# A gated recurrence with a routed expert block on Trainium2: the second expert's rows gathered in quarters and turned by VectorE instead of TensorE

## Chip, cores and metric

The kernel runs on one core of a Trainium2 chip, in one launch, in float32 throughout. The metric is device time in microseconds (us). A run's time is that of the whole execution; beside it stands the span of one profiled execution, from its first to its last instruction.

## What is computed

```python
# q, k, v, a_re, a_im: (4, 8, 768, 48); w_gate (384, 8); w1 (8, 384, 1024); w2 (8, 1024, 384)
for t in range(S):                       # recurrence per batch and head, complex decay
    S = a_n[t] * S + outer(k[t], v[t])   # a_n: a with its magnitude limited to 0.999
    y[t] = q[t] @ S.real
x = y.transpose(0, 2, 1, 3).reshape(3072, 384)
logits = x @ w_gate
e = argmax(logits, axis=1)               # one of 8 experts for each row
gate = softmax(logits)[row, e]
out = gate * (relu(x @ w1[e]) @ w2[e])   # each row through its own expert only
```

## The kernel before, in words

**First part, attention.** The recurrence is computed in six chunks of 128 time steps for each of the four batches, 24 steps in all, on TensorE (PE), with decays and rotations prepared by ScalarE (ACT) and VectorE (DVE). Each step writes 128 finished rows of 384 numbers to a scratch tensor `xd` in device memory and adds to the routing: which expert a row goes to, and its rank there. An explicit table of due times (`WHEN`) gives the order in which a list scheduler places this part.

**Second part, experts.** The eight experts are taken in order of their number of rows, and the order's positions are called places (0 to 7). Place i has room for `CAPS[i]` rows: 448, 416, 416, 408, 400, 384, 376, 360. For each place, in the loop at lines 949 to 961:

- `load_w(i)` (line 588) loads w1 of that expert into `wa` and w2 into `wb`, 1.5 MB each, from SyncE's queue (SP).
- `gather(i, ...)` (line 604) fetches the rows from `xd` into `xg` by indirect DMAs, which GpSimd (POOL) issues one by one.
- `turn(i, ...)` (line 625) puts the rows' 384 features on the partitions, in `xt`.
- `expert(i, ...)` (line 673) computes, per place, `hps` = w1 part times `xt` (8 groups of three products), relu into `ht` (odd groups by ACT, line 686, even ones by DVE, line 688), `yps` = `ht` times w2 for each tile of up to 128 rows, the gate (line 708), and `scatter` (line 654), an indirect DMA of POOL that writes the rows to the output.

In the program a float32 product is two matmul instructions: place 0's last two tiles show 48 of them for 8 groups of three products. A transpose on TensorE is one.

Places come in two kinds, separated by the constant `SQ`. A place below `SQ` is gathered in tiles of 128 whole rows and turned by TensorE: for each of the three blocks of 128 features, one transpose per tile into PSUM (line 643) and one copy to SBUF (line 650, ACT or DVE). A place from `SQ` on is gathered in quarters: four partitions hold a row, 96 numbers in each, so that one indirect DMA brings 32 rows, and one VectorE instruction (line 633) turns the whole place in squares of 32 by 32. Its w1 is loaded in four DMAs of 32 partitions each, since the features then lie in another order over the partitions. The indices of the quarters (`tok4`) come from `squares()` (line 569), which runs for all places whatever `SQ` is.

```python
if i < SQ:                                              # gather, lines 609 to 614
    view, w = xd[0:rows, :], DM
    parts = [(min(P, c1 - t * P), t, tok[:, i, t : t + 1]) for t in range(t0, t1)]
else:
    view, w = xd.rearrange("n (a c) -> (n a) c", a=4), DM // 4
    parts = [(P, j, tok4[:, i, j // 4, j % 4 : j % 4 + 1]) for j in range(4 * t0, -(-c1 // Q4))]
...
if i >= SQ:                                             # load_w, lines 593 to 595
    w = w1[ds(ev, 1)].rearrange("o (a k j) f -> a j (o k) f", a=4, k=KD)
    parts = [(slice(a * Q4, (a + 1) * Q4), w[a]) for a in range(4)]
```

**Order and buffers around the change.** Place 0's first two tiles are worked in the attention part (`early`, line 725), its last two at the start of the loop. The buffers of even and of odd places are two sets of one each (`EP[0]`, `EP[1]`), so place 2's rows can be gathered only when place 0's have been turned. `load_w(1)` waits for place 0's turn (line 948). `turn(i + 1)` is called in the middle of `expert(i)`, behind its relus; the VectorE form is bound to come after the last relu of that place on DVE (`T["held"]`, line 637). VectorE also runs a check of the inputs' range in six pieces (`in_range`, line 916), two passes of 1536 columns each (`junk`, line 923), whose data SP loads into `rc` (line 920). POOL takes its DMAs strictly in the order of the program: place 0's last tiles, place 1's rows, the first scatter, place 2's rows with the second scatter among them, place 3's rows.

Of the kernel before, what the change touches and what calls it, by code (L numbers as in the profile page):

```python
# [22 lines left out]
LN_CAP = math.log(0.999)  # L23
A_MIN = 0.61
T_MAX = 1.5
SQ = 2
Q4 = 32
CAPS = (448, 416, 416, 408, 400, 384, 376, 360)

# [9 lines left out]
def kernel(  # L39
# [40 lines left out]
    def const(shape, name, dt=FP):  # L80
        return cp.tile(shape, dt, name=name)
# [381 lines left out]
    own0 = const([P, 1], "own0", I32)  # L463
    tok = const([P, SQ, CT], "tok", I32)
    tok4 = const([P, E, CT, 4], "tok4", I32)
# [46 lines left out]
    def to_read(f, o):  # L512

        ts(out=o, in0=f, scalar1=-1.0, scalar2=0.0, op0=OP.add, op1=OP.max)
# [37 lines left out]
    def gates_of_places():  # L552
        f = small([P, E, CT], "fi")
        by_place(f, 2)
        to_read(f, f)
        nc.vector.tensor_copy(out=tok, in_=f[:, 0:SQ])
        T["fi"] = f
# [30 lines left out]
    def load_w(i, after=None):  # L588
# [3 lines left out]
        parts = [(slice(0, P), w1[ds(ev, 1)].rearrange("o (k p) f -> p (o k) f", p=P))]  # L592
        if i >= SQ:
            w = w1[ds(ev, 1)].rearrange("o (a k j) f -> a j (o k) f", a=4, k=KD)
# [9 lines left out]
    def gather(i, t0, t1, rows=N):  # L604
# [3 lines left out]
        c1 = min(CAPS[i], t1 * P)  # L608
        if i < SQ:
            view, w = xd[0:rows, :], DM  # L610
# [14 lines left out]
    def turn(i, t0, t1, ps, end=None):  # L625
# [4 lines left out]
        c0, c1 = t0 * P, min(CAPS[i], t1 * P)  # L630
        if i >= SQ:
            j1 = -(-c1 // Q4)
# [615 lines left out]
```

## Time and profile before

| What | us |
|---|---|
| time, median of 3 runs | 550.28 |
| lowest and highest of the 3 | 550.03, 550.4 |
| the profiled execution's own time | 549.1 |
| its span | 547.4 |
| PE busy with matmuls, in the span | 521.0 |
| DVE busy | 288.6 |
| ACT busy | 215.0 |
| POOL busy | 124.0 |

The span begins at 0; times below are microseconds from there. Attention ends at about 270, and the expert part fills the rest. A line of the timeline gives the start, the length, the engine, the line of the kernel, the operation, what it writes and reads, how many instructions were merged, and in brackets how long the engine sat idle before and what released it. A line of the chain of waits gives the start, the length and the work: it follows what ended last back to what released it. "DMA to landing" is the time from the start of an issuing instruction to the moment its data is in place.

### The profile page before, as it was taken

To read this page: it belongs to the slowest core of one execution; us is meant where nothing else is said; L and a number is where in the kernel's file an instruction comes from. 1 tells how busy PE (TensorE), PEld (TensorE's weight loads), DVE (VectorE), ACT (ScalarE), POOL (GpSimd) and SP (SyncE) were. 2 spreads that over 40 slices of the span, in tenths; PEclk is the share of its full clock that TensorE was granted. 3 is DMA by queue.
4 is the path that set the end of the run, shared out by engine and by line. 5 is a ranking of instruction groups with operands and counts; after the bars stand their busy time and mean duration, and the time that the engine had idled before them with its cause. 6 is when DMAs were issued, how large, how long until landed. Compare 5 with 4: busy or idle time off the path is not lost.

```text
span 547.4 us, 8302 instructions
## 1 busy us (share of the span) xinstructions
PE 521.0 (95%) x3166; PEld 372.0 (68%) x3166; DVE 288.6 (53%) x586; ACT 215.0 (39%) x324; POOL 124.0 (23%) x152
## 2 busy tenths in 40 slices
PE   3979979999999999999999999999999999999995
PEld 2756858877888889898885755555555555565663
DVE  5388688678788888697375211271452113111210
ACT  6787888977668974564310110110201111000000
POOL 3000000000000000000034774743716416322101
PEclk9999989999999999999999999999999999999998
DMA  9987692859555935701829976485964334641001
GB/s 164 187 112 109 111 127 33 167 83 175 98 95 99 150 75 110 126 25 29 297 89 308 313 208 152 144 314 108 323 160 145 105 74 140 158 145 42 27 2 42
DMA packets 167495, 73.49 MB, mean 134 GB/s; under 512 B 148861, under 2 KB 160151, under 8 KB 167448
## 3 DMA queue, kind: packets, MB, share of 16 engines
q1 hardware_dynamic: 162744, 63.12, 52.9%
q0 software_dynamic: 4704, 9.76, 6.1%
q8 instruction: 27, 0.44, 0.4%
q14 instruction: 20, 0.16, 0.1%
HBM read 63.34 MB, written 9.73 MB: 134 GB/s over the span
## 4 chain that ended last, share of the span: by engine, by line
PE 84%; issue 6%; DVE 4%; DMA 2%; ACT 2%; POOLq 0%; POOL 0%; ACTq 0%
PE yps L69 22%; PE hps L69 22%; PE tp L332 8%; PE yt L69 7%; PE at L69 7%; PE dk L69 4%; PE cst L69 3%; PE csl L69 3%; PE xb L69 3%; PE warm L69 2%; DMA xg<-xd,tok 1%; PE sp L69 1%; DMA ar<-in_a_re_dram 1%; PE tp L643 1%; DVE fg L283 1%
## 5 line engine op out<-in xcount | busy, mean ns | idle before, releaser
L69 PE MATMUL yps<-wb,ht 128*128 128x384 f32 (+6 forms) x464 | 134.2, 487 | 0.0
L69 PE MATMUL hps<-xt,wa 128*128 128x416 f32 (+7 forms) x432 | 132.7, 465 | 0.0
L69 PEld LDWEIGHTS hps<-xt,wa 128*128 128x128 f32 x432 | 79.8, 190 | 49.8 <-issue 24.8
L69 PEld LDWEIGHTS yps<-wb,ht 128*128 128x128 f32 (+6 forms) x464 | 75.1, 175 | 55.9 <-issue 8.6
L616 POOL DMA_INDIRECT xg<-xd,tok x83 | 85.9, 1035 | 99.3 <-PE tp L332 40.3
L686 ACT ACTIVATE ht<-hps 128x416 f32<-128x416 f32 (+7 forms) x36 | 16.8, 468 | 149.9 <-PE hps L69 138.8
L708 DVE TENSOR_SCALAR y<-yps,gate 128x384 f32<-128x384 f32 (+1 forms) x23 | 14.2, 617 | 101.7 <-PE yps L69 101.7
L69 PE MATMUL at<-qt,kt 96*128 96x128 f32 x384 | 54.0, 280 | 0.3 <-DVE am L340 0.3
L655 POOL DMA_INDIRECT out_dram<-y,row x28 | 29.2, 1044 | 105.4 <-DVE y L708 44.9
L688 DVE TENSOR_SCALAR ht<-hps 128x416 f32<-128x416 f32 (+7 forms) x36 | 18.9, 525 | 63.9 <-PE hps L69 63.7
L261 POOL DMA_DIRECT2D ai<-cd x4 | 3.4, 841 | 210.2 <-ACT R L175 99.5
L69 PEld LDWEIGHTS at<-qt,kt 96*128 96x128 f32 x384 | 47.6, 191 | 4.1 <-issue 1.6
L69 PE MATMUL yt<-am,v 128*48 128x128 f32 x384 | 42.7, 281 | 0.6 <-DVE am L340 0.6
L340 DVE TENSOR_TENSOR am<-at,tri 128x512 f32<-128x512 f32 x48 | 33.0, 688 | 18.6 <-PE at L69 18.5
L69 PE MATMUL yt<-qt,G 96*48 96x128 f32 x320 | 35.7, 274 | 0.0
L718 ACT COPY z<-yps 32x384 f32<-32x384 f32 (+3 forms) x13 | 6.1, 471 | 74.2 <-PE yps L69 74.1
L332 PE MATMUL tp<-ident,K 128*96 128x128 f32 x192 | 33.4, 284 | 1.2 <-DVE K L323 0.8
L69 PEld LDWEIGHTS dk<-v,K 128*96 128x96 f32 x320 | 32.6, 166 | 2.1 <-issue 1.0
L332 PE MATMUL tp<-ident,Q 128*96 128x128 f32 x192 | 33.4, 277 | 0.0
L69 PE MATMUL dk<-v,K 128*96 128x48 f32 x320 | 33.2, 242 | 0.2 <-DVE G L371 0.2
L334 ACT COPY kt<-tp 96x512 f32<-96x512 f32 x48 | 27.9, 582 | 9.9 <-PE tp L332 9.7
L69 PEld LDWEIGHTS yt<-am,v 128*48 128x48 f32 x384 | 24.4, 122 | 8.1 <-DVE am L340 2.0
(170 smaller groups left out, 674.4 us busy)
## 6 DMA issues: line engine op xcount, KB each, us to landing
wb<-in_moe_w_dram SPq DMA_DIRECT2D x8, 1536.0 KB, 7.8
wa<-in_moe_w_dram SPq DMA_DIRECT2D x24, 384.0 KB, 8.5
q<-in_q_dram SPq DMA_DIRECT2D x12, 384.0 KB, 6.7
k<-in_k_dram SPq DMA_DIRECT2D x12, 384.0 KB
v<-in_v_dram SPq DMA_DIRECT2D x12, 384.0 KB, 6.3
xd<-x SPq DMA_DIRECT2D x24, 192.0 KB, 2.2
rc<-in_a_re_dram SPq DMA_DIRECT2D x6, 768.0 KB, 4.9
rc<-in_a_im_dram SPq DMA_DIRECT2D x6, 768.0 KB
```

What stands on the lines that cost most here:

```text
L69: T["mm"] = nc.tensor.matmul(o, lhsT=lhsT, rhs=rhs, start=start, stop=stop, skip_group_check=True)
L283: ts(out=r, in0=cs[:, c0:c1], scalar1=MAGIC, scalar2=MAGIC, op0=OP.add, op1=OP.subtract)
L332: nc.tensor.transpose(out=tp[0:DD, j], in_=X[:, hg * 4 + j], identity=ident)
L334: nc.scalar.copy(out=t[0:DD], in_=tp[0:DD])
L340: tt(out=am, in0=at, in1=bc(tri, 1, 4), op=OP.mult)
L616: nc.gpsimd.indirect_dma_start(out=T["xg", i][0:n, j * w : (j + 1) * w], out_offset=None, in_=view, in_offset=bass.IndirectOffsetOnAxis(ap ...
L643: ins = nc.tensor.transpose(out=tp[:, (t - t0) * P : (t - t0) * P + n], in_=xg[0:n, t * DM + d * P : t * DM + (d + 1) * P], identity=ident ...
L655: ins = nc.gpsimd.indirect_dma_start(out=out, out_offset=bass.IndirectOffsetOnAxis(ap=row[0:n, i, t : t + 1] if to is None else to[0:n], a ...
L686: nc.scalar.activation(out=ht[:, f, c0:c1], in_=ps, func=AF.Relu)
L688: T["held"] = ts(out=ht[:, f, c0:c1], in0=ps, scalar1=0.0, scalar2=None, op0=OP.max)
L708: ts(out=y[0:n], in0=ps[0:n], scalar1=g, scalar2=None, op0=OP.mult)
L718: nc.scalar.copy(out=z[j * w : j * w + n], in_=ps[j * w : j * w + n])
```

## The change

The constant that separates the two kinds of place goes from 2 to 1. Place 1 is then gathered, loaded and turned as places 2 to 7 are; only place 0 keeps whole rows and TensorE.

```diff
 T_MAX = 1.5
-SQ = 2
+SQ = 1
 Q4 = 32
 CAPS = (448, 416, 416, 408, 400, 384, 376, 360)
```

In the built programs the instructions move so:

- PE: the 12 transposes of place 1 are gone, 4 that stood ahead of `hps` of place 0's last two tiles and 8 that stood between this `hps` and its `yps`. Nothing else on PE moves.
- DVE: two copies of 128 by 416 are gone; one transpose of 128 by 1248 stands behind the last relu of place 0 and ahead of the gate of its third tile. The third to sixth pieces of the range check move back by up to a place.
- ACT: one copy of 128 by 416 is gone.
- POOL: 4 gathers of place 1 (128, 128, 128 and 32 rows of 1536 bytes) become 13, each of 128 quarter rows of 384 bytes. They stay where the 4 stood: behind place 0's last tiles, ahead of the first scatter.
- SP: w1 of place 1 is loaded by four DMAs of 32 partitions in place of one of 128. The loads for the range check from the sixth on stand about one place later.
- `tok` has 4 columns in place of 8.

## The prediction on record

> **What bounds the kernel now.** First the engines' shares, then the chain of waits around place 1, then the timelines of PE, POOL and DVE there.
>
> ```profile
> PE 521.0 (95%) x3166; PEld 372.0 (68%) x3166; DVE 288.6 (53%) x586; ACT 215.0 (39%) x324; POOL 124.0 (23%) x152
> ```
>
> PE is busy for 95% of the span, and in the expert part without gaps. The chain (start, length, work) runs over PE from 292 us to the end of place 0 and on:
>
> ```profile
> 292.11 5.16 PE yps L69 x16
> 297.28 0.86 PE tp L643 x5
> 298.13 1.99 PE hps L69 x11
> ```
>
> ```profile
> 303.86 2.27 PE hps L69 x14
> 306.13 1.16 PE tp L643 x8
> 307.29 8.09 PE yps L69 x32
> 315.38 2.64 PE hps L69 x7
> ```
>
> The five transposes at 297.28 are one of place 0 and four of place 1; the eight at 306.13 are place 1's other two blocks. All twelve lie on the chain, with no wait before or after. From 315.38 the chain continues as `hps` and `yps` of one place after the other, each starting where the last ended, up to 541. The last scatter starts at 542.98, behind the last gate at 542.06. So what place 1's turn gives back on PE should arrive at the end, if `xt` of place 1 is ready when PE gets to it.
>
> POOL's timeline shows when rows are asked for:
>
> ```profile
> 288.54 0.94 POOL L616 DMA_INDIRECT xg<-xd,tok  x1 [0.30 <-issue]
> 290.64 1.03 POOL L655 DMA_INDIRECT out_dram<-y,row  x1 [1.17 <-DMA xg<-xd,tok]
> 297.75 1.04 POOL L616 DMA_INDIRECT xg<-xd,tok  x1 [6.08 <-PE tp L643]
> 299.10 2.21 POOL L616 DMA_INDIRECT xg<-xd,tok  x1 [0.30 <-issue]
> 301.61 1.66 POOL L655 DMA_INDIRECT out_dram<-y,row  x1 [0.31 <-issue]
> 303.57 1.03 POOL L616 DMA_INDIRECT xg<-xd,tok  x1 [0.30 <-issue]
> ```
>
> The first is place 1's fourth gather. POOL then is nearly idle until 297.75, when place 0's turn frees the buffer for place 2. The room for nine more gathers is there.
>
> **What the Trainium skill says.** "SBUF — State Buffer", section "Who interferes with whom": a VectorE instruction with two SBUF inputs blocks a GpSimd instruction that reads SBUF. The trace fits, as far as one place can: the range check's passes (two inputs, 1.75 us each) run on DVE from 298.68 to 302.30, and there the gather takes 2.21 us and the scatter 1.66, against 1.00 elsewhere. "DMA: Bandwidth & Descriptors", section "Queues, rings and completion order": each DMA engine takes turns between queues by whole packets, so small gathers wait behind the loads that SP issued. The trace agrees: gathers issued from 324.5 to 332 land in 2.5 to 3.4 us, but those from 306 to 313 in 8.0 to 9.2, under w1's loads. "VectorE: DVE Perf Modes", section "The three transpose paths": VectorE turns only inside squares of 32, which is why the rows must come in quarters; place 2's turn shows it at 1.47 us.
>
> **The change, part by part.** All from the profiled execution: span 547.4, its own time 549.1, which is 1.2 below the median of 550.28. I take differences there and subtract them from the median.
>
> *PE, the eight transposes.* By PE's timeline the first starts at 305.97 and the next `yps` at 307.22: 1.25 us. Without them `yps` follows `hps` directly, as in every later place; it needs the relu of the eighth group only in its last product, 2 us later. Gain 1.25.
>
> *PE, the four transposes.* The five start at 297.21 and `hps` at 298.06, 0.17 each. With one left, `hps` starts at 297.38 and reaches its third product (two instructions per product, 48 in 8.0 us, so 0.167 each) at 298.05, where it needs place 0's last block from DVE. In DVE's timeline the gate runs from 297.31 to 297.93 and the copies follow:
>
> ```profile
> 297.31 0.62 DVE L708 TENSOR_SCALAR y<-yps,gate 128x384 f32<-128x384 f32 x1 [2.53 <-PE yps L69]
> 297.85 0.91 DVE L650 COPY xt<-tp 128x192 f32<-128x192 f32 x2
> ```
>
> The first of the two copies (0.36 alone) ends at 298.21; with 0.04 for the signal PE goes on at 298.25. In the kernel before the third product started at 298.06 + 0.67 = 298.73. Gain 0.48 (0.68 if the copy is no obstacle, 0 if the wait costs as much as the transposes). Sum: 1.25 + 0.48 = 1.73.
>
> *DVE and ACT.* Copies of 0.59, 0.59 and 0.51 us go, one turn of 1.47 comes, on engines that are 53% and 39% busy: nothing, except where PE waits for the turn, next.
>
> *The rows' arrival, the one new wait.* The 13 gathers start at 284.61, where the 4 started; `tok4` is complete at 282.99. At 1.305 us each (place 2's pace) the thirteenth starts at 284.61 + 12 x 1.305 = 300.27. Two pairs of range check passes fall into this stretch, at 291.23 to 294.78 and 298.2 to 302. A pair delayed POOL in the trace by (2.21 - 1.00) + (1.66 - 1.00) = 1.87. With both: 304.0; with none: 300.27. I take 304.0, the slow end. Landing: 6.1 to 9.2 in the stretch 297 to 313. w1 of place 1 now comes in four DMAs; in the same form w1 of place 2 ran at about 210 GB/s, against 400 for the one DMA, so it will occupy the DMA engines from about 300 to 308. The gather at 314.05, as near to the end of such a load, took 6.9. I take 6.9: rows complete at 310.9, turned at 310.9 + 1.47 = 312.4. PE wants them at 315.31 - 1.73 = 313.6. Cover 1.2 us; both slow ends (304.0 + 9.2 + 1.47 = 314.7) cost 1.1. Behind the turn on DVE stand the gate of place 0's third tile (yps ends 310.9 in the new count, read 1.5 late; its PSUM buffer is wanted again after 329) and the relus of place 1, which come after PE's products anyway.
>
> *w1 of place 1.* Four issues take 1.9 us on SP (306.16 for place 2) in place of 0.4, so w2 goes out at about 300.2 in place of 298.8. The four-part load lands 9.9 after its issue at the latest: 298.2 + 9.9 + 1.5 = 309.6, 4 us before PE wants it; w2 follows by about 314, wanted at 330. No cost; from 313.6 on each microsecond would cost one.
>
> *POOL behind it.* The first scatter moves from 290.64 to about 305; the second must wait until the first has landed (6.1 to 7.1 in the trace), with eleven gathers of place 2 behind it. They end near 327, land by 330 to 336, are turned by 338; PE wants them at 347.5. Place 3 has 15 us of cover. No cost.
>
> *Range check.* Its last pieces move from 401 to about 435; the result is first used by PE near 511. No cost. The tail behind the last `yps` is unchanged.
>
> Sum: 550.28 - 1.73 = 548.55, say 548.6 (for the profiled execution 547.4, span 545.7).
>
> **The rivals.**
> *A, the forecast*: the turn is hidden, 548.3 to 548.9.
> *B, part of it comes back*: the thirteenth gather lands between 312.1 and 313.8, PE waits up to 1.7. For it: 9.2 us landings in the trace. Or the four transposes gain nothing: 1.25 only, 549.0. Middle 549.5.
> *C, the rows become the bound; slower than before*: the range check passes hold POOL for their whole 3.6 us per pair, not 1.87: the thirteenth gather starts at 300.27 + 7.2 = 307.5, lands 7.5 later (the landing at 335.1, under place 3's w1) at 315.0, is turned at 316.5, and PE waits 2.9: 548.55 + 2.9 = 551.5. It decides from 313.8 on for the last landing. Against it: the passes at 360 to 364 delayed POOL by only 0.65, the scatter at 394.80 by 0.96.
> *D, more gain*: the copy is early and a wait of PE's weight loads goes too: 548.1 to 548.3.
> That the change doesn't do what it says is excluded: the programs show the 12 transposes gone.
>
> **How the numbers follow.** A 0.62, B 0.18, C 0.15, D 0.05. About 0.2% (1.1 us) is what this measurement can tell from no change, so faster means below 549.18: all of A and D, and the part of B with little loss (0.03), 0.70. Slower means above 551.4: C but for its mildest part, 0.12. The rest, 0.18, is the same. The range: D's lower end, 548.1, and up to 550.8, which takes in all of B (550.3), the bounds of landing and delay, and the mildest of C; 0.13 or so stays above it, little below.
>
> **What would show it.** Right: `hps` of place 0's last tiles followed by `yps` without transposes and a start of place 1's `hps` near 313.6; VectorE's turn of place 1 ending before that; POOL's thirteenth gather starting between 300 and 304. Wrong: PE idle before place 1's `hps`, released by DVE's turn, which itself waited for a DMA (B or C); or PE idle at 297.5 for more than 0.3 us. If place 1's `hps` starts early but the end doesn't move, a later place (2, by the scatter) has become late.

## The result and the profile after

The changed kernel takes 547.97 us in the median of 20 runs (545.18 to 552.79). The kernel before, run beside it, takes 550.15 in the median of 20 (547.66 to 551.92). The ratio is 0.996, with a 95% interval from 0.9942 to 0.9978: faster, by 0.2 to 0.6%. The forecast of 548.6 was 0.6 too high, and the measured time lies 0.13 below the lower end of its range. The profiled execution of the changed kernel took 546.45, with a span of 544.7; the kernel before had a span of 547.4. (The experiments e5 to e8 ran on another, disturbed chip, on which the kernel before itself took 564.85 us in the median; their whole times are set beside nothing but that. Some executions there were slower still, and the ratio given for e7 leaves them out.)

First the shares of the engines, on the page of the changed kernel:

```profile
PE 517.6 (95%) x3154; PEld 369.0 (68%) x3154; DVE 289.2 (53%) x585; ACT 214.6 (39%) x323; POOL 139.1 (26%) x161
```

PE has 12 instructions fewer and POOL nine more, with 15 us more of work. PE's share is what it was. The chain of waits (start, length, work) shows where PE's time went:

```profile
291.33 5.16 PE yps L69 x16
296.50 0.20 PE tp L643
296.70 8.19 PE hps L69 x48
304.89 7.89 PE yps L69 x32
312.78 16.96 PE hps L69 x48
```

Of the five transposes ahead of `hps` one is left, the eight ahead of `yps` are gone, and place 1's `hps` (the last line) follows `yps` with no wait between. The rows came in time, if barely. VectorE's timeline, with the turn and the gate that stands behind it, and PE's, where place 1's `hps` starts:

```profile
310.69 1.48 DVE L633 STREAM_TRANSPOSE xt<-xg 128x1248 f32<-128x1248 f32 x1 [6.39 <-DMA xg<-xd,tok]
312.10 0.58 DVE L708 TENSOR_SCALAR y<-yps,gate 128x384 f32<-128x384 f32 x1
```

```profile
312.71 17.03 PE L69 MATMUL hps<-xt,wa 128*128 128x416 f32 x48
```

The turn waited for the rows' DMA (the bracket) and ended at 312.17, and PE took it up at 312.71. The cover is 0.54 us, where the prediction had 1.2. POOL's timeline shows why the gathers end when they do:

```profile
289.18 1.00 POOL L616 DMA_INDIRECT xg<-xd,tok  x1 [0.30 <-issue]
290.48 2.58 POOL L616 DMA_INDIRECT xg<-xd,tok  x1 [0.31 <-issue]
293.37 1.50 POOL L616 DMA_INDIRECT xg<-xd,tok  x1 [0.30 <-issue]
...
297.77 2.17 POOL L616 DMA_INDIRECT xg<-xd,tok  x1 [0.30 <-issue]
300.25 1.64 POOL L616 DMA_INDIRECT xg<-xd,tok  x1 [0.31 <-issue]
...
303.50 1.00 POOL L616 DMA_INDIRECT xg<-xd,tok  x1 [0.30 <-issue]
```

VectorE's timeline has the range check's passes in the same stretch, here the first two of four:

```profile
290.45 1.75 DVE L923 SCALAR_TENSOR_TENSOR junk<-rc,rc 128x1536 f32<-128x1536 f32 x1
292.24 1.76 DVE L923 SCALAR_TENSOR_TENSOR junk<-rc,rc 128x1536 f32<-128x1536 f32 x1
```

Place 1's thirteen gathers run from 283.97 to the one at 303.50. Four of them are long, and each began under one of these passes. The passes start at 290.45, 292.24, 297.33 and 299.27 and end, counted to the read of their result, 1.68 later, at 292.12, 293.93, 299.00 and 300.95. The first long gather ends at 293.06, 0.94 behind its pass; the others at 294.87, 299.94 and 301.89, 0.94 behind theirs too. So the length of a gather that is caught is the rest of the pass plus 0.94, about what a whole gather takes.

The whole span contains things that have nothing to do with the change, as will be seen, so the experiments are read by a **stretch** inside it: from the start of the sixteen `yps` behind place 0's turn (291.95 before, 291.17 after) to the start of the last gate (542.06 and 539.47). All of the change's work on PE lies in it. The table gives its parts, as differences of start times in the timelines; "turn ends" counts from the sixteen `yps` too.

| kernel | to `hps` of place 0 | to its `yps` | to `hps` of place 1 | to the last gate | stretch | turn ends |
|---|---|---|---|---|---|---|
| before | 6.11 | 9.16 | 8.09 | 226.75 | 250.11 | - |
| after | 5.46 | 8.09 | 7.99 | 226.76 | 248.30 | 21.00 |
| e1, all 12 back | 6.11 | 9.15 | 8.09 | 226.76 | 250.11 | 21.84 |
| e2, 8 back | 5.46 | 9.34 | 8.09 | 226.76 | 249.65 | 20.91 |
| e3, one gather more | 5.46 | 8.09 | 7.98 | 226.76 | 248.29 | 20.97 |
| e4, after again | 5.46 | 8.10 | 7.98 | 226.76 | 248.30 | 21.04 |
| e9, checks held | 5.46 | 8.10 | 7.98 | 226.76 | 248.30 | 19.32 |
| e10, three gathers more | 5.46 | 8.09 | 13.60 | 229.37 | 256.52 | 27.10 |
| e11, before, checks held | 6.11 | 9.16 | 8.08 | 226.76 | 250.11 | - |

The stretch is 1.81 us shorter after the change, and places 2 to 7 take the same time to 0.01 us. So nothing is given back later: the change is worth 1.81 in the place where it was made. Of the other 0.9 us between the two spans, 0.78 lie ahead of the stretch and 0.11 behind it.

### The profile page after: what moved, and what is told of

The parts are those of the page before. It is cut to its first block, busy times and chain, and to the rows that moved or that the text cites. A ratio compares the mean times of both kernels' runs of the same rounds, so it can differ in the third digit from the quotient of the medians.

```text
span 544.7 us, 8306 instructions
## 1 busy us (share of the span) xinstructions
PE 517.6 (95%) x3154; PEld 369.0 (68%) x3154; DVE 289.2 (53%) x585; ACT 214.6 (39%) x323; POOL 139.1 (26%) x161
## 4 chain that ended last, share of the span: by engine, by line
PE 82%; DMA 5%; DVE 4%; ACT 3%; issue 2%; POOLq 0%; SPq 0%; DVEq 0%; ACTq 0%
PE hps L69 23%; PE yps L69 23%; PE tp L332 7%; PE yt L69 7%; PE at L69 7%; PE dk L69 4%; PE cst L69 4%; PE xb L69 3%; PE csl L69 2%; DMA xd<-x 2%; DMA xg<-xd,tok 1%; DMA carry<-cd 1%; PE sp L69 1%; DVE fg L283 1%; DMA out_dram<-y,row 1%
## 5 line engine op out<-in xcount | busy, mean ns | idle before, releaser
L616 POOL DMA_INDIRECT xg<-xd,tok x92 | 100.7, 1095 | 98.1 <-PE tp L332 40.1
L340 DVE TENSOR_TENSOR am<-at,tri 128x512 f32<-128x512 f32 x48 | 33.0, 688 | 18.6 <-PE at L69 18.5
L334 ACT COPY qt<-tp 96x512 f32<-96x512 f32 x48 | 28.1, 586 | 4.3 <-PE tp L332 4.3
```

Of the source, the lines that this page charges most:

```text
L334: nc.scalar.copy(out=t[0:DD], in_=tp[0:DD])
L340: tt(out=am, in0=at, in1=bc(tri, 1, 4), op=OP.mult)
L616: nc.gpsimd.indirect_dma_start(out=T["xg", i][0:n, j * w : (j + 1) * w], out_offset=None, in_=view, in_offset=bass.IndirectOffsetOnAxis(ap ...
```

## The experiments

**e1 and e2: the transposes put back, without the data.** On top of the changed kernel, transposes of the constant identity go back to where place 1's stood: all twelve in e1, only the eight behind `hps` in e2. Nothing reads their result, no copy follows them.

```diff
+    def idle_turns(ps, blocks, end=None):
+        for _ in range(blocks):
+            tp = ps.tile([P, 512], FP, tag="tp", name="tp")
+            for t in range(tiles(1)):
+                n = min(P, CAPS[1] - t * P)
+                ins = nc.tensor.transpose(
+                    out=tp[:, t * P : t * P + n], in_=ident[0:n, 0:P], identity=ident[0:n, 0:n]
+                )
+                behind(ins, [end])
+                T["mm"] = ins
...
         if i >= SQ:
+            if i == 1:
+                idle_turns(ps, 2, T["mm"])
...
+    idle_turns(psG, 1, T["pe"])      # e1 only: ahead of hps of place 0
```

> The changed kernel, with 12 transposes of the identity on TensorE put back where place 1's transposes stood (4 ahead of the products of place 0's last tiles, 8 behind them); their results are not used. Rows, loads and VectorE's turn stay as changed. Theory 1 (only the transposes on TensorE count): from the 16 yps behind place 0's turn to the last gate it takes 250.1 us again as in the kernel before, against 248.3 in the changed one, and the median comes back to within 0.2% of the kernel before. Theory 2 (at least part of the gain comes from the new form of the rows and loads): it stays below 249.5, and the time clearly under the kernel before.

> The same with only the 8 transposes behind the products put back. Theory 1, with the terms of the prediction: 1.25 of the 1.73 come back, so about 249.6 us in the same stretch; the 4 ahead account for the remaining 0.5. Theory 2: no change from the changed kernel beyond 0.3.

The chain of e1:

```profile
293.86 5.16 PE yps L69 x16
299.02 0.20 PE tp L645
299.23 0.65 PE tp L662 x4
299.88 8.00 PE hps L69 x48
307.88 1.16 PE tp L662 x8
309.03 8.09 PE yps L69 x32
317.12 16.96 PE hps L69 x48
```

It is that of the kernel before again, with the same stretch of 250.11. So all 1.81 us are PE's own time in the transposes; the missing copies of ACT and DVE, the other form of w1's load and the gathers add nothing to it. The chain of e2:

```profile
296.50 8.19 PE hps L69 x48
304.69 1.15 PE tp L661 x8
305.85 8.09 PE yps L69 x32
```

The eight cost 249.65 - 248.30 = 1.35: 1.25 up to the start of `yps` (9.34 against 8.09) and 0.10 behind it. The four cost the rest, 250.11 - 249.65 = 0.46: `hps` starts 0.65 earlier without them but then takes 0.19 longer (`yps` follows in 9.34 in place of 9.15). Both stretches, 250.11 and 249.65, are those that were expected.

The whole times tell less. e1 took 549.1 in the median of 14 runs, a ratio of 0.9989 to the kernel before (0.9961 to 1.0016). That interval holds the 1 of the theory, but also 0.9967, which is the change's whole gain; the medians, 549.1 and 550.34, lie 0.23% apart, where 0.2% or less was expected. Its mean, 549.43, lies 1.4 above that of e4 on the same chip, with a standard error of 0.5 (from the scatter of 1.5 of a single run in both). e2 ran once, 547.57, which by itself says nothing.

**e4: the changed kernel itself, under another name.**

> The changed kernel again, for its time against the kernel before in more runs, and for a second profile. Theory 1: the stretch is 248.3 us within 0.1, and what the profile's span differs by lies ahead of the routing, in the first 45 us of a part that both kernels have alike. The ratio of the medians should be nearer to 1.8/550 (0.9967) than the first 0.9960. Theory 2: the ratio stays at 0.9960 or below.

547.73 in the median of 22 runs, ratio 0.9959 (0.994 to 0.9979): the first result again. It didn't move towards the 0.9967 that was expected; by the letter that is theory 2, though the interval holds both. Its profiled execution had a span of 547.4, that of the kernel before, in place of 544.7, with the same stretch of 248.30. The 2.7 us lie ahead of it, 1.9 of them in the first 45 us: the first copy `ys` of attention's result stands at 43.97 here and at 42.09 in the first profile. Most of the rest lies at the routing, where PE waited 1.28 in place of 0.36, so the expectation that all of it lies ahead of the routing was met only in part. PE's timeline of e4 at the start:

```profile
27.80 0.88 PE L69 MATMUL cst<-ai,tri_turn 128*128 128x384 f32 x2 [1.29 <-ACT ai L175]
30.34 2.90 PE L69 MATMUL cst<-ai,tri_turn 128*128 128x384 f32 x4 [1.66 <-DVE fg L284]
```

And that of the changed kernel's first profile:

```profile
27.03 0.88 PE L69 MATMUL cst<-ai,tri_turn 128*128 128x384 f32 x2 [1.29 <-ACT ai L175]
29.58 1.53 PE L69 MATMUL cst<-ai,tri_turn 128*128 128x384 f32 x4 [1.66 <-DVE fg L284]
```

The same four products, behind the same wait, took 2.90 and 1.53. The view by stretches gives the granted clock (the third figure here) for 30 to 35 us of e4:

```profile
30.00:35.00 5.00, 4.66 (x23) 0.68 0.50 69
```

In the first profile it is 1.00 there. The Trainium skill, "TensorE: Matmul & The Clock Gate", section "Part 1: The HAM clock gate", says that the clock is set from free-running windows of about 3.4 us of activity, so that the point where it changes varies from run to run; two waits of 1.29 and 1.66 with 0.9 of work between them, which cost the clock in one execution and not in another, fit that; no run here tests it. e1 and e10 have 0.68 and a first `ys` at 43.94 and 43.98; e2, e3 and e9 have 1.00 and 42.05 to 42.10. The kernel before (43.65) had a clock of 1.00, but its warm-up products ended 2 us later (26.7 against 24.5). So one profile against another differs by up to 2 us that belong to the execution and not to the kernel.

**e3: one extra gather.** If the rows are the next bound, a later last gather must show when the cover is used up. One quarter gather into a tile that nobody reads goes ahead of place 1's rows.

```diff
+        if i == 1:
+            for x in range(1):                       # 3 in e5 and e10, 5 in e6
+                spare = EP[1].tile([P, DM // 4], FP, tag=f"spare{x}", name="spare")
+                nc.gpsimd.indirect_dma_start(
+                    out=spare, out_offset=None, in_=view,
+                    in_offset=bass.IndirectOffsetOnAxis(ap=tok4[:, i, 0, 0:1], axis=0),
+                    bounds_check=view.shape[0] - 1, oob_is_err=False,
+                )
         for n, j, ap in parts:
```

> The changed kernel with one more gather of 128 quarter rows, into a tile that nobody reads, ahead of the 13 of place 1. In the changed kernel VectorE's turn ended 0.54 us before TensorE needed it. If the turn's cover is what the trace shows, 1.3 us more of POOL makes TensorE wait 0.6 to 0.9 us in front of place 1's products, and the stretch grows from 248.3 to about 249.1. If the rows wait for the DMA engines and not for POOL's issues, the last landing doesn't move and neither does the stretch.

Nothing moved (stretch 248.29, one run of 546.7): the expectation of a later turn failed. The last gather started 12.33 us behind the sixteen `yps` in both kernels. Of the extra 1.3 us, 1.06 went into time that POOL had lost anyway; for the rest, POOL was 0.26 further ahead of PE in this execution. In POOL's timeline of e3 the gather that the first pass caught is

```profile
290.59 1.00 POOL L624 DMA_INDIRECT xg<-xd,tok  x1 [0.30 <-issue]
291.89 1.52 POOL L624 DMA_INDIRECT xg<-xd,tok  x1 [0.30 <-issue]
```

1.52 long in place of 2.58: the pass began at 290.80, the gather begun just ahead of it went through, and the caught one had only the rest to wait for, ending 0.93 behind the pass (292.48).

**e5, e10 and e6: three and five extra gathers.** The scheduler also put the first scatter ahead of place 1's thirteenth gather (e5, e10), or of its last three (e6), so POOL has 5.2 us more to issue ahead of the last one in e5 and e10 (three gathers of 1.3 and a scatter of 1.3).

> As e3, with three more gathers (each into a tile of its own that nobody reads) ahead of place 1's. In e3 the one more gather was absorbed: POOL's thirteenth gather of place 1 started at the same distance behind place 0's turn, since POOL had lost the time behind VectorE's range check passes anyway. Three are 3.9 us, of which that can absorb 1.3 to 2. If the cover of 0.5 us is real, VectorE's turn ends 1.9 to 2.6 us later, TensorE waits 1.4 to 2.1 us ahead of place 1's products, and the stretch grows from 248.3 to 249.7 to 250.4. If the rows have more room than the trace shows, it stays at 248.3.

> The changed kernel with three extra quarter gathers into a tile that nothing reads, ahead of place 1's rows, once more on another chip. Theory (cover 0.5 us, from there microsecond for microsecond): place 1's hps waits for the turn by 3.1 us, as in the first run of it (2.5 to 3.5), and the distance from the sixteen yps to the last gate is 248.3 + 3.1 = 251.4, within 0.5. Rival (the first run's wait came from the disturbed chip alone): the wait is below 1 us and the distance below 249.3.

> As e5, with five more gathers: 6.5 us of POOL. Theory: slope one beyond the cover, so 2.6 us more than e5, the stretch at 252.3 to 253, slower than the kernel before (250.1). This is the rival C of the prediction brought about on purpose: the rows as the bound.

PE's timeline of e5, where place 1's `hps` starts, and then that of e10:

```profile
316.18 17.03 PE L69 MATMUL hps<-xt,wa 128*128 128x416 f32 x48 [3.06 <-DVE xt L641]
```

```profile
321.43 19.64 PE L69 MATMUL hps<-xt,wa 128*128 128x416 f32 x48 [5.54 <-DVE xt L641]
```

Both waits are for the turn, which itself waited for the rows' DMA in both, so that the rows are the next bound is shown, on two chips: rival C's wait is real, and the change is one scatter and a few gathers away from it. (It was brought about by extra gathers here; that the passes alone bring it about, as C had it, no run shows.) The waits follow from the turn's end: 24.62 us behind the sixteen `yps` in e5 and 27.10 in e10, less 21.54, when PE asks, gives 3.08 and 5.56. All three expectations of the wait were missed: in e5 3.06 in place of 1.4 to 2.1, in e6 8.51, which is 5.45 more than e5 in place of 2.6, and in e10 5.54 in place of 2.5 to 3.5. In e5 the scatter that moved ahead adds 1.3, which the expectation had left out. In e10 the gathers began 0.43 later relative to PE than in e5, one pass held a gather 0.86 longer (2.51 against 1.65), and the last took 8.07 to the turn in place of 6.88. In e6, with its turn's end at 30.06, a pass and the landing added to the gathers in the same way (2.58 against e5's 1.65, 8.38 against 6.88).

What none of the theories had: the theory was microsecond for microsecond, but in e10 the 5.54 us cost 8.22. The view by stretches gives for e10, behind the wait (length, PE busy and its instructions, granted clock, the DMA engines' share and GB/s):

```profile
320.00:325.00 5.00, 3.57 (x5) 0.50 1.04 234
325.00:330.00 5.00, 5.00 (x13) 0.83 0.91 306
330.00:335.00 5.00, 5.00 (x16) 1.00 0.18 51
```

After the wait PE ran at half its clock, and came back to 1.00 within the second slice, so place 1's `hps` took 19.64 against 17.03 after the change. These 2.6 and the wait make up the 8.22. e6, after its 8.51, has 0.50 for the five us behind the wait too and took 19.52; e5, after 3.06, kept 1.00 and took 17.03. The Trainium skill has this: "TensorE: Matmul & The Clock Gate", section "HAM oscillation — how this bites in real kernels", says that gaps of PE over about 3.4 us bring its clock down to half, and these three waits fall on the sides of that figure where they should. So does a later one of 4.80 in e5 (the granted clock is 0.66 and 0.65 in the two slices from 340 to 350). But a single long wait isn't the only way: the clock fell at the start of e4, and in e8, on the disturbed chip, it is 0.55 from 320 to 325, behind a row of waits of which none was over 1.6.

The whole times: e10 557.65 (one run; 550.15 for the kernel before there); e5 565.22 and e6 572.26 on the other chip. The stretches that were expected of e5 and e6 (249.7 to 250.4, 252.3 to 253) can't be read there: theirs are 266.87 and 274.98, but e8, which lacks the change, has 266.27 too. Up to place 1's `hps` the same kernels take the times of the table, but for the waits named.

**e7 and e9: the range check held back.** The lengthened gathers were put down to VectorE's passes. In these kernels the loads of the check's data wait for place 0's last relu, so that no pass runs beside the gathers.

```diff
-            nc.sync.dma_start(out=t, in_=s[:, j * RW : (j + 1) * RW])
+            ins = nc.sync.dma_start(out=t, in_=s[:, j * RW : (j + 1) * RW])
+            tc.add_manual_dep(ins.ins, T["held0"].ins.name, SYNC, reason="rows first")
...
+        if i == 0:
+            T["held0"] = T["held"]
```

> The changed kernel, with the loads of the range check (3.9 MB from 282 us on) made to wait until the last relu of place 0. If they are what place 0's last rows wait for, those rows land 3 to 4 us after their issue and not 7, TensorE's wait ahead of place 0's turn (0.60 us in the changed kernel's profile) goes, and the distance from the last copy of yt to the 16 yps falls from 23.2 to 24.6 to about 22.6 in every execution. The range check's passes no longer delay POOL either: the thirteenth gather of place 1 starts at about 300 in place of 303.5, and VectorE's turn ends some 4 us earlier without a gain in time. Sum: 0.6 to 2 us less than the changed kernel, about 547. If the rows wait for POOL's and the queue's own time, the distance stays.

> The changed kernel with the loads of the range check held back until place 0's last relu, once more, because the first run of it fell on a chip on which the kernel before itself took 14 us longer. Theory (the rows of place 1 come in time whatever POOL meets; cover 0.5 us): place 1's gathers, no longer lengthened by VectorE's passes, start 2 to 4 us earlier, so VectorE's turn ends at least 2 us before TensorE wants it; the distance from the sixteen yps behind place 0's turn to the last gate is 248.3 less the 0.2 that hps of place 0 waits, so 248.1 to 248.3, and the median is within 1 us of the changed kernel's. Rival (the range check is better early: put back, it falls on a stretch where VectorE is needed): the distance is 249 or more and the median above the changed kernel's by 1 us or more, with VectorE's relus late and TensorE waiting for them.

POOL's timeline of e9, in the stretch in which four gathers were long:

```profile
290.18 1.00 POOL L616 DMA_INDIRECT xg<-xd,tok  x1 [0.30 <-issue]
291.48 1.00 POOL L616 DMA_INDIRECT xg<-xd,tok  x1 [0.30 <-issue]
...
297.99 1.00 POOL L616 DMA_INDIRECT xg<-xd,tok  x1 [0.30 <-issue]
...
300.59 1.00 POOL L616 DMA_INDIRECT xg<-xd,tok  x1 [0.30 <-issue]
```

All are 1.00 long, and the thirteenth starts 9.09 us behind the sixteen `yps` in place of 12.33. That the passes lengthen them is thereby shown, and the page "SBUF — State Buffer" of the Trainium skill, section "Who interferes with whom", agrees: it names a VectorE instruction with two SBUF inputs and a GpSimd instruction that reads SBUF as a pair that contends. The held loads themselves aren't the cause: in the changed kernel the gathers from 283.97 to 289.18 ran beside them and took 1.00. And where a gather of e9 meets a pass later, at 364.50, it takes 1.90 and ends 0.95 behind it. But VectorE's timeline gives

```profile
309.34 1.48 DVE L633 STREAM_TRANSPOSE xt<-xg 128x1248 f32<-128x1248 f32 x1 [4.70 <-DMA xg<-xd,tok]
```

and so the turn ends only 1.68 earlier, not 3.2: the last gather took 8.75 from its start to the turn, against 7.19. It was issued 2.8 behind the first issue of w1's load, in place of 6.1; that this is the reason is likely, but not shown. The cover grows to 2.2 us, and since 0.54 was enough, the time stays: 547.68 in the median of 20 runs, ratio to the kernel before 0.9958 (0.9935 to 0.998), the changed kernel's own within the interval. The rival, a loss, is refuted on this chip. On the other one, e7 had been expected to gain 0.6 to 2 us; it took 572.68 against 564.85 of the kernel before (ratio 1.0113, 1.0085 to 1.0141). Its profile has waits of up to 7 us on DVE in place 0 which it ascribes to no work of this core, but so has e8's (8.9 and 18.6 on DVE). Why that kernel lost more there is open.

**e8 and e11: the same in the kernel before.**

> The kernel before with the same hold on the range check's loads. The distance from the last copy of yt to the 16 yps falls to about 22.6 as in e7, and the stretch behind them stays at 250.1 us: the hold and the change of the second place add up, since they touch different waits.

> The kernel before with the same loads held back in the same way. Theory: the passes only delay place 0's last rows, for which TensorE waited 0.84 us in the kernel before, and nothing else ahead of place 1, so the distance from the last copy of attention's result to the sixteen yps goes from 23.3 to about 22.5, the distance from the sixteen yps to the last gate stays 250.1 within 0.2, and the time falls by 0.8 at most. Rival (passes put back cost elsewhere): the distance to the last gate is over 250.6.

e11: 550.05 in the median of 12 runs, ratio 0.9998 (0.9971 to 1.0025), stretch 250.11: no change, and no loss. PE's wait of 0.84 for place 0's last rows is gone, as expected, but the sixteen `yps` didn't come earlier (24.01 behind the last copy `ys`, against 23.27; about 22.5 was expected, which failed): in this execution PE had waited 1.43 for the routing's `oh` at 275.6, where the first profile shows no wait of note. In all thirteen profiles this distance, less PE's waits for `oh` and for place 0's last rows, is 22.4 to 22.7. So the hold does take the rows' wait away, and the other wait, which differs from one execution to the next, hides it. The same holds for e7 and e9: e7's distance, expected to fall to 22.6, was 23.30 with 0.72 of waiting for `oh`, and e9's was 23.43 with 0.85. e8 took 566.77 in one run, on the other chip, with a distance of 23.18 and a stretch of 266.27, where 22.6 and 250.1 were expected: both were missed.

## Why the prediction was right, and where its range was not

- *The eight transposes, 1.25.* Right: 1.25 by e2 up to `yps`, and 0.10 more inside `yps` and its end.
- *The four, 0.48 of 0.68, the rest lost to the wait for place 0's last copy.* Right: 0.46; 0.65 earlier and 0.19 lost. The view of `wa` has PE idle for 0.2 inside this `hps`, until DVE's copy of `xt`.
- *The sum, 1.73.* 1.81 measured. e1 shows that nothing else contributes.
- *The thirteenth gather at 304.0, 19.39 behind the first; passes cost 1.87 a pair.* 19.53; the two pairs cost 2.08 and 1.81. The slow end was the right one to take.
- *Landing 6.9; cover 1.2.* 7.19, and 0.54. The cover lost 0.14 by the first gather's start, 0.14 by the passes, 0.29 by the landing, and 0.1 because PE came earlier. None of it cost time, but it was half of the cover.
- *w1 of place 1 in four parts, 4 us of cover.* Its four issues run from 297.4 to 299.1 and the landing takes 9.2, so 308.3 at the latest, 4.4 ahead of PE. Right.
- *POOL behind it: place 2 turned by 338.* At 331.0, with 15.6 us in hand. Right in its sense; the price was too careful. *Room for nine more gathers:* not in the gap that the prediction pointed to, which is 6.1 us long while nine gathers take 11.7; the rest of them pushed place 2's rows back, and it was the cover of place 2 that held. *Range check to about 435:* its last pass ends at 432.
- *Rival B* didn't happen. *Rival C* didn't happen either, but e5, e6 and e10 show that the rows become the bound. Its price of the passes, 3.6 a pair, was too high (2.08 and 1.81), and a microsecond for each of wait holds only for short ones: e5's 3.06 cost 3.1 up to the end of place 1's `hps`, e10's 5.54 cost 8.2.

**The step that failed** is that of the range: "D's lower end, 548.1", with "little below". The cases A to D differed only in what the change does, and the median of 550.28 and the changed kernel's coming median entered as if they were exact. The prediction did put at 1.1 us what the measurement can tell from no change, but used that for the three classes and not for the range. The three runs that it had agree within 0.4 us; the 20 to which they belong go from 547.66 to 551.92, so their closeness was luck, and bad luck.

Measured against the forecast, 548.55 less 547.97, is 0.58. Of that, 0.08 is the size of the gain (1.81 in place of 1.73) and 0.17 the base: the mean of all 86 runs of the kernel before, those on the disturbed chip left out, is 550.11. The other 0.33 is within what a median of 20 such runs scatters by. These 86 runs have a standard deviation of 1.64, the first 20 of the changed kernel 2.08. So a mean of three of the one is uncertain by 1.64 / √3 = 0.95, of 20 of the other by 2.08 / √20 = 0.47, together 1.06 (a median by somewhat more): that alone, above and below 548.55, should have been in the range. That the result fell 0.13 outside of it and not just inside is chance.

The sources of the scatter are seen in the profiles: PE's clock and warm-up in the first 45 us (up to 1.9 from one execution of a kernel to another), and waits around the routing and place 0's last rows (23.0 to 24.6 between the last `ys` and the sixteen `yps`). Over all runs, again without that chip, the means are 550.11 (86 runs) and 548.06 (42 runs of the changed kernel and e4), a difference of 2.05 with a standard error of 0.33. That agrees with 1.81; a few tenths of gain or loss ahead of the stretch would not show.

## What to carry to other kernels

Where one engine is busy without gaps, an instruction taken from it is worth its time in the stream, and an idle engine can do the work for nothing as long as its input lands before it is wanted: write down that cover as a number, since here 0.5 us of 21 were left. Measure such a gain in a stretch between two fixed events of the trace, which repeated to 0.01 us on every chip but the disturbed one where whole executions scatter by 1.6, and let a range contain that scatter, which three runs don't show.

## What was not expected of the hardware

- The price of a wait on PE isn't always its length: 5.54 us of idleness cost 8.22, since the granted clock was 0.50 afterwards; 3.06 cost its length (e10, e5).
- A gather that begins under a two-input VectorE pass ends about 0.94 us behind that pass wherever it began, so that one more gather ahead of the pass cost almost nothing (e3).
- Gathers issued 3.2 us earlier brought the rows only 1.7 earlier: from the last one's start to the turn it took 8.75 in place of 7.19 us, beside w1's load (e9).
- The same four products at the start, behind the same wait, took 1.53 or 2.90 us (e4).
